# Second row tiles of four experts share one 128-row tile in a sparse attention, mixture-of-experts and feed-forward kernel

## The chip, the cores and the metric

The kernel runs on one core of a Trainium2 chip. The metric is the device time of one execution in microseconds; of several executions the median is given. The engines are named as the profile names them: PE is TensorE, PEld its weight loads, DVE VectorE, ACT ScalarE, POOL GpSimd, SP SyncE; a "q" behind a name is that engine's queue of issues.

## What is computed

```python
attn = attention(q, k, v)            # 4 x 8 heads, 576 positions, 64 wide; half local, half strided
x = attn as [2304, 512]
do = x @ w_skip > 0
e = argmax(x[do] @ w_gate, axis=1)   # 8 experts
gate = softmax(x[do] @ w_gate)[e]
x[do] += gate * (relu(x[do] @ w1[e]) @ w2[e])      # w1: 512 x 1024, w2: 1024 x 512
h = x @ w_in                         # 512 x 2048
out = maximum(0.01 * h, h) @ w_out   # 2048 x 512
```

With the inputs that the reference draws, 1016 of the 2304 rows go to an expert: 113, 110, 157, 141, 148, 152, 107 and 88 for experts 0 to 7.

## The kernel before

There are three stages. In the first, 43 attention units (19 strided, 24 local) go through a pipeline of small steps, one step of the loop for each: scores, exponentials, transposes, products with the values and with the router's weights (`s_scores` to `s_table`). Each row of the result (two halves with their router sums, 530 numbers) goes to DRAM, `x2_d`. From ranks within each expert a table `places` of row numbers is built: 160 places (`CAP`) for each of 8 experts, in two tiles of 128 and 32 (`TS`, `TN`); empty places hold a number out of bounds, and a gather or scatter leaves them out. Idle products (`keep_warm`, on zeros) stand at a few places in PE's order.

In the second stage the experts run one after the other. For each, `gather_rows` fetches the two row tiles by two indirect DMAs on POOL (L636), one expert ahead; `turn_in` (L643) transposes them on PE, four transposes for each tile, and ACT and DVE each copy one half out of PSUM; for eight slices `f` of the hidden width come `first_layer` and, two slices later (`LAG`), `second_layer`, on 160 columns; `copy_out` and `turn_out` (L677) bring the result back, again four transposes for each tile; `expert_out` multiplies it with the gate (`gates`, L619), adds it to the gathered rows and scatters them (L692). Meanwhile DVE, ACT and POOL decode the dense weights, step by step (`decode_tick`). The last expert is joined with the dense layers' start (`last_second` to `last_place`): its rows are put into the first 256 rows' operand by products with a selection matrix, while its scatters and the loads of the next rows (`load_rows`, L611) go on.

In the third stage the dense layers run on tiles of 256 and then 512 rows (`mm1`, `mm2`); a copy and a DMA for each 128 rows bring out the result (L934).

PE's order is the order of the code; on the other engines a scheduler sets it, and `behind_pe` holds an instruction behind another.

Of the kernel before, what the change touches and what calls it, by code (L numbers as in the profile page):

```python
# [36 lines left out]
TS = (slice(0, P), slice(P, CAP))  # L37
TN = tuple(t.stop - t.start for t in TS)
NBLK = -(-(NT - CAP) // CAP)
OC = NBLK * CAP  # L40
# [12 lines left out]
SZ = B * SR - GU * (NSU - 1)  # L53
WARMS = {0: 2, 1: 2, 2: 1}
FC1 = F // P
# [21 lines left out]
WARM_END = 8  # L77
WARM_MID = (4, 1)
VT_LATE = 1
# [20 lines left out]
def tile_sparse_attention_moe_ffn(ctx: ExitStack, tc: tile.TileContext, sb, vs, lb, vl, mk, tris, cst, ranks, wrb, w1, w2, dw, out):  # L100
# [14 lines left out]
    x2_d = dp.tile([NT, XW], F32, name="x2_d")  # L115
    x_parts = dram_disjoint_views(x2_d, 2 * E)

# [88 lines left out]
    acc = const.tile([P, 1, E], BF16, name="acc")  # L206
    idx = const.tile([P, 2, E], U32, name="idx")
    rr_t, m2_t, cm_t = (const.tile([P, NLU], F32, name=n) for n in ("rr_t", "m2_t", "cm_t"))
# [36 lines left out]
    with ExitStack() as actx:  # L245
# [98 lines left out]
        def s_weigh(i):  # L344

            z = st[i]
            nk = z["nk"]
            vw = ps_c.tile([P, 4, P], F32, tag="c", name="vw")[:nk, :2]
            for p in range(2):
                c = (p + (2 if units[i][0] == "s" else 0)) * 2 * NR  # L350
                nc.tensor.matmul(vw[:, p, :NW], z["vt"][:, p, :], wr_sb[:, c:c + NW], start=True, stop=True)  # L351
            ins = nc.scalar.copy(z["v"][:nk, :, D + 1:].rearrange("p (a b) e -> p a b e", a=2),
                                 vw[:, :, :2 * NR].rearrange("p a (b e) -> p a b e", b=2))
            if i < GRP:
                behind_pe(ins, eng=mybir.EngineType.Activation)

# [171 lines left out]
        def s_table(i):  # L528
# [21 lines left out]
            nc.vector.tensor_reduce(places, ix.rearrange("p t a e -> p t e a"), AX.X, ALU.add)  # L550
            nc.vector.tensor_copy(idx, places)

        stages = ((s_scores, 0), (s_load, LL), (s_transpose, 2), (s_weigh, 1),
                  (s_values, 3), (s_join, 3), (s_place, 5), (s_table, 6), (s_logits, 4))
        for step in range(LL, NU + 6):
            for fn, lag in stages:
                if 0 <= step - lag < NU:
                    fn(step - lag)
            keep_warm(WARMS.get(step, 0))
            if step == NU + 2:  # L560
# [55 lines left out]

    gate_of, pairs = {}, {}

    def gates(key, pair):  # L619
        l4 = pair[:, :, :XW].rearrange("p t (h w) -> p t h w", h=2)  # L620
        lg = mp.tile([P, 2, E], F32, tag="glg", name="glg")
        nc.vector.tensor_tensor(lg, l4[:, :, 0, 4 * D:4 * D + E], l4[:, :, 1, 4 * D:4 * D + E], ALU.add)
        nmx = mp.tile([P, 2], F32, tag="gmx", name="gmx")
        nc.vector.tensor_reduce(nmx, lg, AX.X, ALU.max, negate=True)
        nc.vector.tensor_tensor(lg, lg, nmx.unsqueeze(2).to_broadcast([P, 2, E]), ALU.add)
        nc.scalar.activation(lg, lg, AF.Exp)
        es = mp.tile([P, 2], F32, tag="ges", bufs=3, name="ges")
# [3 lines left out]
        gate_of[key] = es  # L631

    def gather_rows(e):
        rows, pairs[e] = row_pair()
        for t, n in enumerate(TN):
            ins = nc.gpsimd.indirect_dma_start(  # L636
                out=rows[t][:n, :XW], out_offset=None, in_=x_parts[2 * e + t][:, :],
                in_offset=bass.IndirectOffsetOnAxis(ap=idx[:n, t, e:e + 1], axis=0),
                bounds_check=NT - 1, oob_is_err=False)
            behind_pe(ins, dep=GDEP)  # L640
        return rows

# [42 lines left out]

    def expert_out(po, rows, toks, gate, e=None):
        for t, n in enumerate(TN):
            ins = nc.vector.scalar_tensor_tensor(x_of(rows[t])[:n], po[t][:n].rearrange("p (h w) -> p h w", h=2),
                                                 gate[:n, t:t + 1], x_of(rows[t])[:n], ALU.mult, ALU.add)
            if e == E - 1:  # L690
                behind_pe(ins)
            nc.gpsimd.indirect_dma_start(  # L692
                out=(x2_d if e is None else x_parts[2 * e + t])[:, :],
                out_offset=bass.IndirectOffsetOnAxis(ap=toks[t], axis=0),
                in_=rows[t][:n, :XW], in_offset=None, bounds_check=NT - 1, oob_is_err=False)
# [11 lines left out]

    def last_turn(po, c2, ot, out):

        (nc.vector.tensor_copy if c2 else nc.scalar.copy)(ot[:, 2 * c2:2 * c2 + 2], po)  # L710
        for t, n in enumerate(TN):
            for c in (2 * c2, 2 * c2 + 1):
                nc.tensor.transpose(out[t][:n, c * P:(c + 1) * P], ot[:, c, TS[t]], ident)

    def last_gate(out, gate, c2, ys):

        cs = slice(c2 * NTT, (c2 + 1) * NTT)
        for t, n in enumerate(TN):
            yh, yl = ys[t]
            nc.scalar.activation(yh[:n, cs], out[t][:n, cs], AF.Identity, scale=gate[:n, t:t + 1])  # L720
            nc.vector.scalar_tensor_tensor(yl[:n, cs], out[t][:n, cs], gate[:n, t:t + 1], yh[:n, cs].bitcast(F32),
                                           ALU.mult, ALU.subtract)

    def last_place(pt, c2, ys, sel, x):

        for c in (2 * c2, 2 * c2 + 1):
            for t, n in enumerate(TN):
                for k, y in enumerate(ys[t]):
                    nc.tensor.matmul(pt[:, c % 2, :], y[:n, c * P:(c + 1) * P], sel[:n, t, :],  # L729
                                     start=False, stop=(t + k == 2 and c % 2 == 1))  # L730
# [20 lines left out]
    LAG = 2  # L751
    rows = {0: gather_rows(0)}
    keep_warm(WARM1)
# [9 lines left out]
    with tc.If(nblk > 0):  # L763
# [24 lines left out]
        with tc.For_i(0, E, 1) as e:  # L788
            with tc.For_i(0, nblk, 1) as k:
# [10 lines left out]
                for f in range(FC1):  # L800
# [4 lines left out]
                    second_layer(gpo, b2, first_layer(b1.rearrange("p (c n) -> p c n", c=KC), gxt), f == FC1 - 1)  # L805
                gates(None, gpair)
                expert_out(turn_out(copy_out(gpo), ps_c, "c"), grows, toks, gate_of.pop(None))

    keep_warm(WARM2)
    xt_of = {0: turn_in(rows[0])}  # L810
    gs, pos, ots = {}, {}, {}
    for j in range(len(seq) + LAG):
        if j < len(seq):
# [9 lines left out]
            if e + 1 < E and f == GF:  # L823
                rows[e + 1] = gather_rows(e + 1)
        for e in list(ots):
            expert_out(turn_out(ots.pop(e), ps_c, "c"), rows.pop(e),
                       [idx[:n, t, e:e + 1] for t, n in enumerate(TN)], gate_of.pop(e), e)
        if LAG <= j < len(seq) + LAG - TAIL:
            e, f = seq[j - LAG]
            second_layer(pos[e], r2s[(j - LAG) // 2][:, f % 2], gs.pop(j - LAG), f == FC1 - 1)  # L830
            if f % 2:
                load_w2((j - LAG) // 2 + 3)
            if f == FC1 - 1:
                ots[e] = copy_out(pos.pop(e))
        if j < len(seq):
            e, f = seq[j]
            if f == 2:
                gates(e, pairs.pop(e))
            if e == E - 1 and f == FC1 - 1:
                sel = mp.tile([P, 2, NTT], F32R, tag="sel", bufs=1, name="sel")  # L840
                for t in range(2):
                    behind_pe(nc.vector.tensor_scalar(sel[:, t, :], rank_sb, places[:, t, E - 1:], None, ALU.is_equal))
            if e + 1 < E and f == 5:
                xt_of[e + 1] = turn_in(rows[e + 1])
    nxt = load_rows(0, dq_last[-1])
    e = E - 1
    po = pos.pop(e)
# [9 lines left out]
    last_second(0, 2)  # L857
    ot = mp.tile([P, KC, CAP], F32, tag="ot", name="ot")
    out_t = [ps_a.tile([P, DM], F32, tag="a", name="pto") for t in TN]
# [3 lines left out]
    last_second(1, 0)  # L863
    last_turn(po[0], 0, ot, out_t)
    last_gate(out_t, gate_of[e], 0, ys)
    pt = turn_next(nxt, 0)
    last_second(1, 2)
    last_place(pt, 0, ys, sel, x0)
    pt = turn_next(nxt, 1)
    last_turn(po[1], 1, ot, out_t)  # L870
    last_gate(out_t, gate_of[e], 1, ys)
    ahead = [open_h(NTT)]
    mm1(ahead[0], 0, x0, (0, 1))
    last_place(pt, 1, ys, sel, x0)
    expert_out(out_t, rows.pop(e), [idx[:n, t, e:e + 1] for t, n in enumerate(TN)], gate_of.pop(e), e)
    ahead.append(open_h(NTT))
# [18 lines left out]
    for j in range(len(fseq) + LAG):  # L895
# [22 lines left out]
        if j >= LAG:  # L918
# [5 lines left out]
            if f == FC2 - 1:  # L924
                po = pos.pop(i)
                for t in ts:
# [9 lines left out]
                    nc.sync.dma_start(out[a:a + P, :], y)  # L936
        if j < len(fseq):
# [145 lines left out]
```

## Time and profile before

| | us |
|---|---|
| median of 3 runs | 695.44 |
| the runs | 693.45, 695.44, 696.0 |
| the profiled execution | 693.17 |
| its span, first to last instruction | 691.1 |
| PE busy | 684.9 |
| attention, until about | 117 |
| experts, about | 123 to 272 |
| dense layers, from about | 288 |

Busy time is read against the stage it lies in: an engine that is half busy over the span can be full in one stage. A transpose or product has a record with its whole latency, so the distance from one group's start to the next says what a group costs; the chain of waits gives these distances. An idle stretch is told with the event that ended it.

### The profile page before, as it was taken

The page shows a single profiled execution, that of the slowest core. Times are in us where ns is not written, and L with a number is a line of the kernel's source. Part 1 is how long each engine was busy: PE and PEld are TensorE (multiplying, and loading weights), DVE is VectorE, ACT ScalarE, POOL GpSimd, SP SyncE. Part 2 cuts the span into 40 slices and gives each one's busy share as a digit, 9 for nine tenths or more (in the row PEclk, how much of TensorE's full clock was granted, in tenths as well). Part 3 has the DMA queues.
Part 4 walks back from the last instruction along what each step waited for, and adds up shares of the span by engine and source line. Part 5 has one row for each costly group of instructions (what it writes and reads, how often), then busy time and mean ns, then how long its engine had stood idle before and what let it go on. Part 6 is the DMA issues. An engine that isn't in the chain of part 4 may idle for free.

```text
span 691.1 us, 11591 instructions
## 1 busy us (share of the span) xinstructions
PE 684.9 (99%) x4336; PEld 596.5 (86%) x4336; DVE 334.4 (48%) x971; ACT 259.9 (38%) x685; POOL 115.3 (17%) x170
## 2 busy tenths in 40 slices
PE   9999999999999999999999999999999999999997
PEld 6999986899999999888888888888888888888886
DVE  4788886244445553589988322223222232222221
ACT  5677763223323333355545223223232222232222
POOL 1333323133333332123332000000000000000000
PEclk9999999999999999999999999999999999999999
DMA  8978772688898887253332021000110000010001
GB/s 324 357 252 277 243 291 59 204 285 296 298 308 292 299 292 264 75 194 115 107 96 57 0 94 62 0 1 1 31 38 24 1 1 0 1 61 1 1 0 61
DMA packets 36558, 92.71 MB, mean 134 GB/s; under 512 B 6016, under 2 KB 8160, under 8 KB 36496
## 3 DMA queue, kind: packets, MB, share of 16 engines
q1 hardware_dynamic: 31568, 82.79, 35.6%
q0 software_dynamic: 4640, 8.99, 4.0%
q8 instruction: 35, 0.57, 0.3%
q14 instruction: 27, 0.22, 0.1%
q10 hardware_dynamic: 288, 0.13, 0.1%
HBM read 80.69 MB, written 12.32 MB: 135 GB/s over the span
## 4 chain that ended last, share of the span: by engine, by line
PE 97%; DVE 1%; issue 1%; DMA 0%; ACT 0%; POOL 0%; POOLq 0%; DVEq 0%; ACTq 0%
PE ph L743 28%; PE pf L749 28%; PE ph L656 10%; PE po L669 9%; PE o L384 5%; PE pt L362 3%; PE vw L351 3%; PE sc L334 3%; PE sc L331 2%; PE ptx L596 1%; PE pto L682 1%; PE ptx L648 1%; PE pw L219 1%; PE po L853 1%; PE pts L729 0%
## 5 line engine op out<-in xcount | busy, mean ns | idle before, releaser
L749 PE MATMUL pf<-wouth,gp 128*128 128x512 f32 x576 | 190.5, 390 | 0.0
L910 DVE TENSOR_TENSOR tg<-tg,ph 128x512 f32<-128x512 f32 (+1 forms) x80 | 50.7, 633 | 171.6 <-ACT tg L909 171.5
L749 PEld LDWEIGHTS pf<-wouth,gp 128*128 128x128 f32 x576 | 108.2, 188 | 22.2 <-DVE gp L916 0.2
L743 PE MATMUL ph<-th,winh 128*128 128x512 f32 (+1 forms) x320 | 119.4, 373 | 0.0
L743 PE MATMUL ph<-tl,winh 128*128 128x512 f32 (+1 forms) x320 | 118.1, 369 | 0.1
L743 PE MATMUL ph<-th,winl 128*128 128x512 f32 (+1 forms) x320 | 118.0, 369 | 0.0
L749 PE MATMUL pf<-woutl,gp 128*128 128x512 f32 x288 | 112.3, 390 | 0.0
L909 ACT ACTIVATE tg<-ph 128x512 f32<-128x512 f32 (+1 forms) x80 | 44.2, 553 | 178.2 <-PE ph L743 178.1
L656 PE MATMUL ph<-xt,r 128*128 128x160 f32 x512 | 80.6, 301 | 0.4 <-ACT xt L650 0.3
L669 PE MATMUL po<-g,r 128*128 128x160 f32 x480 | 75.0, 299 | 0.0
L656 PEld LDWEIGHTS ph<-xt,r 128*128 128x128 f32 x512 | 72.7, 190 | 1.5 <-ACT xt L650 0.7
L916 DVE TENSOR_TENSOR gp<-tg,gp 128x512 fp32r<-128x512 f32 (+1 forms) x80 | 51.0, 638 | 42.7 <-ACT gp L915 42.6
L743 PEld LDWEIGHTS ph<-th,winh 128*128 128x128 f32 x320 | 60.3, 188 | 10.7 <-DVE tl L598 0.4
L743 PEld LDWEIGHTS ph<-tl,winh 128*128 128x128 f32 x320 | 60.3, 189 | 10.4 <-DVE tl L734 0.3
L743 PEld LDWEIGHTS ph<-th,winl 128*128 128x128 f32 x320 | 60.3, 188 | 10.1
L669 PEld LDWEIGHTS po<-g,r 128*128 128x128 f32 x480 | 68.3, 190 | 0.1
L915 ACT CAST gp<-tg 128x512 fp32r<-128x512 f32 (+1 forms) x80 | 46.1, 578 | 50.7 <-DVE tg L910 50.3
L749 PEld LDWEIGHTS pf<-woutl,gp 128*128 128x128 f32 x288 | 54.1, 188 | 10.7
L340 ACT ACTIVATE p_t<-sc,mx 96x128 f32<-96x128 f32 (+2 forms) x172 | 48.3, 361 | 10.9 <-DVE mx L337 8.2
L658 ACT ACTIVATE g<-ph 128x160 f32<-128x160 f32 x64 | 19.2, 301 | 60.1 <-PE ph L656 60.1
L384 PE MATMUL o<-vt,pts 128*96 128x104 f32 (+4 forms) x344 | 39.6, 258 | 0.1
L151 ACT ACTIVATE w<-raw 128x256 f32<-128x256 f32 x64 | 27.8, 434 | 29.6 <-POOL woutl L169 18.9
(130 smaller groups left out, 774.9 us busy)
## 6 DMA issues: line engine op xcount, KB each, us to landing
r<-in_w SPq DMA_DIRECT2D x64, 512.0 KB, 4.7
raw<-in_dw SPq DMA_DIRECT2D x64, 256.0 KB, 4.1
gt<-in_lb SPq DMA_DIRECT2D x12, 704.0 KB, 6.3
gt<-in_sb SPq DMA_DIRECT2D x7, 756.0 KB, 6.6
row<-x_d SPq DMA_DIRECT2D x9, 530.0 KB, 4.5
out<-ys SPq DMA_DIRECT2D x18, 256.0 KB, 2.1
vt<-in_vl SPq DMA_DIRECT2D x12, 296.0 KB, 6.3
vt<-in_vs SPq DMA_DIRECT2D x9, 296.0 KB, 5.7
```

The source lines that it names most:

```text
L151: behind_pe(nc.scalar.activation(wf, raw[:, :, 1].bitcast(F32), AF.Abs))
L334: nc.tensor.matmul(sc[:, a, p], z["q"][r, p], z["k"][r, p], start=False, stop=p == 1)
L340: nc.scalar.activation(p_t[:nq, h, :nk], sc[:, h % 2, h // 2], AF.Exp, bias=mx[:, h % 2, h // 2:h // 2 + 1], scale=scale)
L384: nc.tensor.matmul(o[:nq, h, :w], z["pts"][:nk, h, :nq], z["v"].rearrange("p a b -> p (a b)")[:nk, h * VP:h * VP + w], start=True, stop=True)
L656: nc.tensor.matmul(ph, w[:, c, :], xt[:, c, :], start=c == 0, stop=c == KC - 1)
L669: nc.tensor.matmul(po[c // 2][:, c % 2], w[:, c * P:(c + 1) * P], g, start=False, stop=end and c % 2 == 1)
L743: nc.tensor.matmul(ph, dense_w[k, f][:, c, :], v[:, c % 2], start=c + i == 0, stop=c == KC - 1 and i == 2)
L749: nc.tensor.matmul(po[t], a[:, s], x, start=(first and i == 0), stop=(last and i == 2))
L909: nc.scalar.mul(t1, ph, 0.01)
L910: ins = nc.vector.tensor_tensor(g, t1, ph, ALU.max)
L915: nc.scalar.copy(gh, g)
L916: nc.vector.tensor_tensor(gl, g, gh.bitcast(F32), ALU.subtract)
```

## The change

The second tiles of four experts become one tile of 128 rows, each expert with 32 of them (`EG`, `NG`, `SEC`): `gidx` holds its row numbers, made by four small products from `places` and a cast. The first expert of a group gathers it, transposes it and keeps the transposed rows (`xg`); each expert's operand gets a slice of 32 columns by a copy. Behind the second layer, the last 32 columns go into `otg`, which is transposed back, multiplied with its gates and scattered behind the group's last expert. Fixed places (`SLOTS`, `GSLOTS`) hold the rows. Of the idle products those of steps 1 and 2 (`WARMS`) and one ahead of the last table products (`WARM_MID`) go, one is added ahead of the small products; those of step 0 use another pool. The copy of the router's products (`s_weigh`) isn't held behind ACT's last instruction any more. The gates are held behind PE. The last copy of the kernel is made in two halves, on DVE and ACT, each with its own DMA.

```diff
+EG = 4
+NG = E // EG
+SEC = CAP - P
+SLOTS = (0, 2, 3, 4, 0, 2, 3, 4)
+GSLOTS = (1, 5)
...
-WARMS = {0: 2, 1: 2, 2: 1}
+WARMS = {0: 2}
...
-WARM_MID = (4, 1)
+WARM_MID = (4, 0)
...
-            if i < GRP:
-                behind_pe(ins, eng=mybir.EngineType.Activation)
...
-            nc.vector.tensor_copy(idx, places)
+            nc.vector.tensor_copy(idx, places[:, 0])
+            keep_warm(1, ps_s, "s")
+            gi = ps_b.tile([P, NG], F32, tag="b", name="gi")
+            for k in range(EG):
+                nc.tensor.matmul(gi[k * SEC:(k + 1) * SEC], ident[:SEC, :SEC],
+                                 places[:SEC, 1].rearrange("p (g k) -> p k g", k=EG)[:, k], start=True, stop=True)
+            nc.vector.tensor_copy(gidx, gi)
+            nc.scalar.copy(gplaces, gi)
...
+    def gather_rows(e):
+        gather(slot(SLOTS[e]), idx[:, e:e + 1], e)
+        g = e // EG
+        if e % EG == 0:
+            gather(slot(GSLOTS[g]), gidx[:, g:g + 1], E + g)
+
+    def turn(rows):
+        pt = ps_c.tile([P, KC, P], F32, tag="c", name="ptx")
+        for c in range(KC):
+            nc.tensor.transpose(pt[:, c], rows[:, x_cols(c)], ident)
+        return pt
...
+    def turn_rows(e):
+        xt = mp.tile([P, KC, CAP], F32, tag="xt", name="xt")
+        pt = turn(slot(SLOTS[e]))
+        g, k = divmod(e, EG)
+        if k == 0:
+            pg = turn(slot(GSLOTS[g]))
+            nc.vector.tensor_copy(xt[:, :, P:], pg[:, :, :SEC])
+        nc.scalar.copy(xt[:, :2, :P], pt[:, :2])
+        nc.vector.tensor_copy(xt[:, 2:, :P], pt[:, 2:])
+        if k == 0:
+            xgs[g] = mp.tile([P, KC, P], F32, tag="xg", name="xg")
+            nc.vector.tensor_copy(xgs[g][:, :, SEC:], pg[:, :, SEC:])
+        else:
+            nc.vector.tensor_copy(xt[:, :, P:], xgs[g][:, :, k * SEC:(k + 1) * SEC])
+        return xt
...
+    def put_out(e, c2, po, ot):
+        g, k = divmod(e, EG)
+        if k == 0 and c2 == 0:
+            otgs[g] = mp.tile([P, KC, P], F32, tag="otg", bufs=1, name="otg")
+        a, b = (nc.scalar.copy, nc.vector.tensor_copy)[::-1 if c2 else 1]
+        cs = slice(2 * c2, 2 * c2 + 2)
+        a(ot[:, cs], po[:, :, :P])
+        b(otgs[g][:, cs, k * SEC:(k + 1) * SEC], po[:, :, P:])
...
+        while done:
+            e, ot = done.pop(0)
+            rows_out(turn_back(ot), slot(SLOTS[e]), idx[:, e:e + 1], e, e)
+            g, k = divmod(e, EG)
+            if k == EG - 1:
+                rows_out(turn_back(otgs.pop(g)), slot(GSLOTS[g]), gidx[:, g:g + 1], E + g, E + g)
...
-                    nc.scalar.copy(y, po[t])
+                    if end and t == ts[-1]:
+                        cs = slice(0, NTT), slice(NTT, DM)
+                        nc.vector.tensor_copy(y[:, cs[0]], po[t][:, cs[0]])
+                        nc.sync.dma_start(out[a:a + P, cs[0]], y[:, cs[0]])
+                        nc.scalar.copy(y[:, cs[1]], po[t][:, cs[1]])
+                        nc.scalar.dma_start(out[a:a + P, cs[1]], y[:, cs[1]])
```

The order of PE where expert 0's result is turned back, between products of expert 1 (`ph` is the first layer, `po` the second, `pto` the transposes; an `r_` is a weight tile), before:

```order
L656 MATMUL ph<-xt,r_2928 128x160 x4
L682 MATMUL pto<-ident,ot 128x128 x4
L682 MATMUL pto<-ident,ot 32x128 x4
L669 MATMUL po_2964<-g,r_2913 128x160 x2
L669 MATMUL po_2965<-g,r_2913 128x160 x2
```

and with the change:

```order
L724 MATMUL ph<-xt,r_2928 128x160 x4
L699 MATMUL pto<-ident,ot 128x128 x4
L737 MATMUL po_2964<-g,r_2917 128x160 x2
L737 MATMUL po_2965<-g,r_2917 128x160 x2
L724 MATMUL ph<-xt,r_2928 128x160 x4
```

Four of the eight transposes are gone; where expert 3 is turned back, four of `otg` stand in their place. The transposes in (`ptx`) lose their four of 32 rows in the same way.

The order of PE at the end of attention, where the last table products (`ix`) are closed and idle products (`pw`) follow, with the change (before, the rows of `gi` and one pair of `pw` aren't there):

```order
L551 MATMUL ix<-oa,rm 32x16
L554 LDWEIGHTS zero
L554 MATMUL ix<-zero 128x32
L226 LDWEIGHTS zero
L226 MATMUL pw<-zero 128x512
L560 MATMUL gi<-places,ident 32x2 x4
L226 LDWEIGHTS zero
```

The four products of `gi` stand ahead of the twelve idle products that cover the gathers, and wait for `places`.

The order of DVE around the transposes into expert 1 (`w` are decoding steps), before:

```order
L162 SCALAR_TENSOR_TENSOR w<-raw,w 128x256
L650 COPY xt<-ptx 128x320
L156 TENSOR_SCALAR w<-w 128x256
L160 TENSOR_SCALAR w<-w 128x256
L161 SCALAR_TENSOR_TENSOR w<-raw,w 128x256
L162 SCALAR_TENSOR_TENSOR w<-raw,w 128x256
```

and with the change:

```order
L161 TENSOR_SCALAR w<-w 128x256
L677 COPY xt<-ptx 128x2x128
L165 TENSOR_SCALAR w<-w 128x256
L166 SCALAR_TENSOR_TENSOR w<-raw,w 128x256
L167 SCALAR_TENSOR_TENSOR w<-raw,w 128x256
L682 COPY xt<-xg 128x4x32
```

The operand's copy is smaller and stands behind one decoding step more; the slice of the group's rows comes four steps behind that.

## Rows read from the trace of the kernel before

**Rows 1.** The page: busy time with share and instructions; granted clock by slice.

```profile
PE 684.9 (99%) x4336; PEld 596.5 (86%) x4336; DVE 334.4 (48%) x971; ACT 259.9 (38%) x685; POOL 115.3 (17%) x170
...
PEclk9999999999999999999999999999999999999999
```

**Rows 2.** Stage table: stretch, length, busy time per engine, granted clock, DMA share, GB/s.

```profile
123.00:272.00 149.00, 148.64 (x1109) 145.52 (x1108) 73.65 (x199) 45.91 (x144) 47.98 (x56) 1.00 0.84 285
```

**Rows 3.** Chain of work, 136 to 157 us: start, length, engine, line.

```profile
136.56 1.28 PE ph L656 x8
...
146.81 0.87 PE pto L682 x8
147.68 1.09 PE po L669 x8
...
155.29 0.80 PE ptx L648 x8
156.09 1.01 PE ph L656 x6
```

**Rows 4.** Waits of PE's weight loads, 117 to 272 us: in total, times, longest.

```profile
PEld ptx L648 <- issue: 1.3, 8, 0.2
```

**Rows 5.** Opening: timeline of weight loads and one DMA issue, then that issue's landing.

```profile
7.77 0.13 PEld L331 LDWEIGHTS <-mk_sb 64*126 64x126 bf16 x2 [0.42 <-DVE mx L337]
...
9.50 0.12 PEld L219 LDWEIGHTS <-zero 128*128 128x128 bf16 x1
10.08 0.13 PEld L331 LDWEIGHTS <-mk_sb 64*126 64x126 bf16 x2 [0.46 <-issue]
...
12.63 0.13 PEld L331 LDWEIGHTS <-mk_sb 64*126 64x126 bf16 x2
...
5.48 0.36 SPq L292 DMA_DIRECT2D gt<-in_sb  x1
...
gt<-in_sb SPq DMA_DIRECT2D x1, 756.0 KB, 6.6
```

**Rows 6.** Chain of work, its first piece.

```profile
1.00 3.17 PE pw L219 x7
```

**Rows 7.** Turn to the experts: timeline of POOL and PEld, then both gathers' landings.

```profile
118.68 1.13 POOL L636 DMA_INDIRECT row<-x_d,idx  x1 [2.24 <-issue]
120.12 0.94 POOL L636 DMA_INDIRECT row<-x_d,idx  x1 [0.31 <-issue]
...
124.34 0.57 PEld L656 LDWEIGHTS ph<-xt,r 128*128 128x128 f32 x4 [0.68 <-ACT xt L650]
125.16 0.98 PEld L656 LDWEIGHTS ph<-xt,r 128*128 128x128 f32 x7 [0.26 <-DVE xt L650]
...
row<-x_d,idx POOLq DMA_INDIRECT x1, 3.8
...
row<-x_d,idx POOLq DMA_INDIRECT x1, 2.8
```

**Rows 8.** Into the dense layers: timeline; landings of two scatters, one row load.

```profile
287.16 0.88 POOL L692 DMA_INDIRECT x_d<-row,idx  x1 [0.30 <-DVE tl L734]
...
289.14 1.43 SPq L611 DMA_DIRECT2D row<-x_d  x3
...
294.56 1.02 PEld L596 LDWEIGHTS ptx<-ident,row 128*128 128x128 f32 x8
...
x_d<-row,idx POOLq DMA_INDIRECT x1, 2.7
...
x_d<-row,idx POOLq DMA_INDIRECT x1, 1.9
...
row<-x_d SPq DMA_DIRECT2D x1, 530.0 KB, 4.8
```

**Rows 9.** The end: timeline of ACT; and the group of ACT's 256-column copies.

```profile
687.47 0.58 ACT L934 COPY ys<-pf 128x512 f32<-128x512 f32 x1 [0.72 <-PE pf L749]
...
L733 ACT CAST th<-pts 128x256 fp32r<-128x256 f32 x2 | 0.7, 372 | 2.4 <-PE pts L729 1.9 <-DVE tl L734 0.5
```

More of the change, by code (lines that the diff above doesn't have):

```diff
@@ L558, in tile_sparse_attention_moe_ffn @@
                     fn(step - lag)
-            keep_warm(WARMS.get(step, 0))
+            keep_warm(WARMS.get(step, 0), ps_b, "b")
             if step == NU + 2:
@@ L630, in gates @@
         nc.vector.reciprocal(es, es)
-        gate_of[key] = es
-    def gather_rows(e):
[L634 to L641, printed above, removed]
+        gate_of.update((k, es[:, t:t + 1]) for t, k in enumerate(keys))
@@ new lines, in slot, with gather @@
+    def slot(i):
+        return row_pairs[i // 2][:, i % 2]
+    def gather(r, tok, part):
+        ins = nc.gpsimd.indirect_dma_start(
+            out=r[:, :XW], out_offset=None, in_=x_parts[part][:, :],
+            in_offset=bass.IndirectOffsetOnAxis(ap=tok, axis=0), bounds_check=NT - 1, oob_is_err=False)
+        behind_pe(ins, dep=GDEP)
+    def gather_rows(e):
+        gather(slot(SLOTS[e]), idx[:, e:e + 1], e)
+        g = e // EG
+        if e % EG == 0:
+            gather(slot(GSLOTS[g]), gidx[:, g:g + 1], E + g)
@@ new lines, in tile_sparse_attention_moe_ffn, with turn_back @@
+    otgs = {}
+    def put_out(e, c2, po, ot):
[6 more added lines that the diff above has]
+        b(otgs[g][:, cs, k * SEC:(k + 1) * SEC], po[:, :, P:])
+    def turn_back(ot):
+        p = ps_c.tile([P, DM], F32, tag="c", name="pto")
+        for c in range(KC):
+            nc.tensor.transpose(p[:, c * P:(c + 1) * P], ot[:, c], ident)
+        return p
@@ L643, in turn_in, with rows_out @@
+    def rows_out(p, r, tok, key, part, last=False):
+        ins = nc.vector.scalar_tensor_tensor(x_of(r), p.rearrange("p (h w) -> p h w", h=2), gate_of.pop(key),
+                                             x_of(r), ALU.mult, ALU.add)
+        if last:
+            behind_pe(ins)
+        nc.gpsimd.indirect_dma_start(
+            out=x_parts[part][:, :], out_offset=bass.IndirectOffsetOnAxis(ap=tok, axis=0),
+            in_=r[:, :XW], in_offset=None, bounds_check=NT - 1, oob_is_err=False)
     def turn_in(rows):
@@ L684, in turn_out, with expert_out @@
         return po
-    def expert_out(po, rows, toks, gate, e=None):
+    def expert_out(po, rows, toks, gate):
         for t, n in enumerate(TN):
[L688 to L691, printed above, removed]
+            nc.vector.scalar_tensor_tensor(x_of(rows[t])[:n], po[t][:n].rearrange("p (h w) -> p h w", h=2),
+                                           gate[t][:n], x_of(rows[t])[:n], ALU.mult, ALU.add)
             nc.gpsimd.indirect_dma_start(
-                out=(x2_d if e is None else x_parts[2 * e + t])[:, :],
-                out_offset=bass.IndirectOffsetOnAxis(ap=toks[t], axis=0),
+                out=x2_d[:, :], out_offset=bass.IndirectOffsetOnAxis(ap=toks[t], axis=0),
                 in_=rows[t][:n, :XW], in_offset=None, bounds_check=NT - 1, oob_is_err=False)
@@ L751, in tile_sparse_attention_moe_ffn @@
     LAG = 2
-    rows = {0: gather_rows(0)}
+    gather_rows(0)
     keep_warm(WARM1)
@@ L833, in tile_sparse_attention_moe_ffn @@
             if f == FC1 - 1:
-                ots[e] = copy_out(pos.pop(e))
+                ot = mp.tile([P, KC, P], F32, tag="ot", name="ot")
+                for c2, p in enumerate(pos.pop(e)):
+                    put_out(e, c2, p, ot)
+                done.append((e, ot))
         if j < len(seq):
@@ L837, in tile_sparse_attention_moe_ffn @@
             if f == 2:
-                gates(e, pairs.pop(e))
+                if e == 0:
+                    gates((0, E), row_pairs[0])
+                else:
+                    gates((e,), slot(SLOTS[e]).unsqueeze(1))
+            if f == 3 and e and e % EG == 0:
+                gates((E + e // EG,), slot(GSLOTS[e // EG]).unsqueeze(1))
             if e == E - 1 and f == FC1 - 1:
                 sel = mp.tile([P, 2, NTT], F32R, tag="sel", bufs=1, name="sel")
-                for t in range(2):
-                    behind_pe(nc.vector.tensor_scalar(sel[:, t, :], rank_sb, places[:, t, E - 1:], None, ALU.is_equal))
+                for t, at in enumerate((places[:, 0, E - 1:], gplaces[:, NG - 1:])):
+                    behind_pe(nc.vector.tensor_scalar(sel[:, t, :], rank_sb, at, None, ALU.is_equal))
             if e + 1 < E and f == 5:
-                xt_of[e + 1] = turn_in(rows[e + 1])
+                xt_of[e + 1] = turn_rows(e + 1)
     nxt = load_rows(0, dq_last[-1])
+    gate = gate_of[E - 1], gate_of[E + NG - 1]
     e = E - 1
@@ L863, in tile_sparse_attention_moe_ffn @@
     last_second(1, 0)
-    last_turn(po[0], 0, ot, out_t)
-    last_gate(out_t, gate_of[e], 0, ys)
+    last_turn(po[0], 0, ots, out_t)
+    last_gate(out_t, gate, 0, ys)
     pt = turn_next(nxt, 0)
@@ L874, in tile_sparse_attention_moe_ffn @@
     last_place(pt, 1, ys, sel, x0)
-    expert_out(out_t, rows.pop(e), [idx[:n, t, e:e + 1] for t, n in enumerate(TN)], gate_of.pop(e), e)
+    rows_out(out_t[0], slot(SLOTS[e]), idx[:, e:e + 1], e, e, last=True)
+    rows_out(out_t[1], slot(GSLOTS[NG - 1]), gidx[:, NG - 1:], E + NG - 1, E + NG - 1, last=True)
     ahead.append(open_h(NTT))
```

71 lines of the change are left out of this document (36 added, 35 removed).

## The prediction

> **What bounds the kernel now.** I read the page first. TensorE (PE) is busy for 99% of the span, and the granted clock is in its top tenth in all 40 slices [rows 1]. The chain of waits that ended last runs through PE's instructions, one behind the other, as its piece in [rows 3] shows. So time is lost or won where PE works, and only there; the other engines count where PE waits for them. Next the stage table: while the experts run (123 to 272 us) PE is busy for 148.64 of 149 us, VectorE (DVE) for 73.65, ScalarE (ACT) for 45.91, and the DMA engines for 0.84 of theirs at 285 GB/s [rows 2]. The reader should see that PE is full, DVE and ACT are about half idle or more, and the DMA engines are the only other resource that is near its end. Then the chain inside one expert: from one expert's first product after its transposes (136.56) to the next one's (156.09) it takes 19.53 us, without a gap [rows 3].
>
> **The change part by part.** The experts get 113, 110, 157, 141, 148, 152, 107 and 88 rows, so the second row tiles hold 0, 0, 29, 13 and 20, 24, 0, 0: a group tile carries 42 rows, then 44.
>
> *Transposes back.* Eight take 0.87 us, for both tiles, so four take 0.435 [rows 3]. Experts 0, 1, 2, 4, 5 and 6 now turn back one tile; 3 and 7 still two. Saved: 6 x 0.435 = 2.61 us.
>
> *Transposes in.* Eight take 0.80 us, and the eight products behind them 1.28 us until the next group starts (136.56 to 137.84), where a group of eight otherwise takes 1.09 (147.68): 0.99 in all [rows 3]. The extra 0.19 I lay to the 32-row tile: the weight loads of these transposes wait eight times for "issue", 1.3 us together, which is once for each expert, where the operand changes from 128 rows to 32 [rows 4]. With four 128-row transposes left (0.435) an expert saves 0.555; six of them (1, 2, 3, 5, 6, 7) save 3.33. Expert 4 has eight of 128 rows: 0.99 - 0.87 = 0.12. If the 0.19 stays, it is 6 x 0.365 - 0.07 = 2.12 instead of 3.45.
>
> So the experts' stage gives 6.06 us (at least 4.73). What is added there is covered: the group copies, an extra copy on each engine for every expert, lie on DVE and ACT, and the 32-row multiply-add on DVE goes. The transposed rows are wanted only after the layers 6 and 7, 4 x 1.09 us later; without that cover each late microsecond would cost PE one. POOL loses one gather and one scatter for six of eight experts.
>
> *Opening.* Three idle products go. Those of step 1 cost nothing, since PE waits for the scores' buffer anyway. That of step 2 stands between 9.50 and 10.08, with its load of 0.12 and 0.46 us of "issue" behind it: 0.58 [rows 5]. But the scores of unit 4 start at 12.63, and their operands, issued at 5.48, land 6.6 us later, at 12.08 [rows 5]: 0.55 us is the most. I take 0.45, as the semaphore needs some of it; the lower end is 0.
>
> *The turn to the experts.* One idle product ahead of the last table products goes; a 512-column product took 3.17 / 7 = 0.45 us at the start, at the 1.2 GHz level [rows 6], so 0.2 at 2.4 GHz, and the gathers go out 0.2 earlier. Added are one idle product and four small products that build the group's indices (on PE, then a cast on DVE); POOL is busy with the first gather until 119.81 and issues the second at 120.12, so this wait is covered. The first gather carries 113 rows and lands 3.8 us after its start; the second carried no row and landed after 2.8 [rows 7]. Now it carries 42: 2.8 + 42/113 = 3.2 us, so 123.1 with the 0.2. Then four transposes (0.435), their own length (0.2) and a small DVE copy (0.3, estimates): the first layer starts at about 124.1. Before, it started at 124.34, waited for DVE's half of the copy until 125.16 and finished 0.54 later, at 125.70 [rows 7]; the gate's work stood ahead of that copy and now stands behind it. New end: 124.1 + 1.09 = 125.2, a gain of 0.5. Bounds: 3.8 us for the gather gives -0.1, 2.8 us gives 0.7 (PE's own idle products then set the start).
>
> The Trainium skill ("DMA: Bandwidth & Descriptors", Anatomy of one DMA) prices a GpSimd transfer at 2.0 us and its bytes at 436 GB/s; 42 rows of 2,120 bytes would be 0.2 us in place of my 0.4, and with the same for the scatter below the time would come out at 688.1.
>
> *Into the dense layers.* The last scatter moved no row: issued at 287.16, it landed 1.9 us later, and the row loads go out at once behind it, at 289.14. The second of them, just after 289.6, takes 4.8 us, so 294.45; PE loads its first transpose at 294.56 [rows 8]. The slack is 0.1. Now the scatter carries 44 rows; one of 88 rows took 2.7 us: 1.9 + 0.8 x 44/88 = 2.3, and PE stalls for 0.3. Bounds: 0 and 0.7.
>
> *The end.* The last copy takes 0.58 us on ACT; 256 columns take 0.37 [rows 9]. Halves on two engines and two queues: 0.2 earlier (0 to 0.4).
>
> Sum: -6.06 - 0.45 - 0.5 - 0.2 + 0.3 = -6.9 us (-3.9 to -7.7). The profiled execution took 693.17 us (span 691.1, 2.1 around it), 2.3 below the median of the runs shown. From it the sum gives 686.3; from the median of 695.44, 688.5. I forecast the median: **688.5 us**.
>
> **The rivals.** *The clock falls in the opening.* Fewer idle products leave PE idle for over half a microsecond near 7 us, just when it has become fast. For it speaks that the first seven products run at 0.45 us [rows 6]; against it that PE is full from then on and no slice shows a lower clock [rows 1]. If the low level came back for as long as these seven took (3.2 us), half of that, 1.6 us, would be lost: 690.1, still faster. The Trainium skill ("TensorE: Matmul & The Clock Gate", Part 1) says that the clock is halved after idleness and restored by sustained work, which speaks for keeping such products; no run here shows it as yet.
>
> *The DMA engines become the experts' bound.* They are at 0.84 [rows 2]; weights for an expert must come in 18.5 us and not 19.5, so 0.89. If 285 GB/s were all that this mix of transfers gives, the 6.06 would be kept back by waits for weights, and only the -0.85 of the other terms is left: 694.6, no change. Against it: no weight load is named by any PE wait.
>
> *The change does less than it says:* the saved transposes come back as waits for the copies of group rows, in part, and 2 to 3.4 us remain: 692 to 693.4, no change to measure.
>
> *Slower: the slice copy holds up each expert.* DVE's copy of a slice into the next expert's operand stands in its queue behind decoding steps, which wait for ACT and for their loads. From 4.6 us behind the transposes (4 x 1.09 and the two zero products) each microsecond is PE's. For a loss over 3.5 us seven experts would have to stall for 1.5 us each, so the copy would have to come 6.1 us late: 699. Against it: DVE is idle for half of the stage [rows 2].
>
> **How the numbers follow.** About 0.5% (3.5 us) can be told from no change here. My forecast has 0.80, the clock 0.05, the DMA bound 0.06, the weak form 0.06, the slice copy 0.03. Faster: 0.80 + 0.05 = 0.85; same: 0.12; slower: 0.03. The range goes from 693.17 - 7.7 = 685.5 to 695.44 - 3.9 = 691.5; it holds the first two cases, and leaves out about 0.15.
>
> **What would show it.** Right: the chain from expert to expert at 18.5 us where no group is turned, the group of eight products behind the transposes at 1.09; the first layer done near 125 us; unit 4's scores near 12.2 us; a PE wait of about 0.3 us ahead of the transposes near the start of the dense layers; PE's idle products short by three. Wrong: weight loads for the experts waiting on a DMA (the second rival), weight loads of the first layer waiting for a copy on DVE (the fourth), idle products at double length after 7 us (the first), or the transposes' saving coming out at 4.7 because the 0.19 is not the 32-row tile's.

## The result and the profile after

The changed kernel takes **687.85 us** (median of 6, 687.62 to 688.41) where the kernel before, in the same group of runs, takes 694.57 (median of 6, 692.76 to 696.0): a ratio of 0.9913, 95% interval 0.99 to 0.9927. In a second group it was 688.05 to 693.50, 0.9923 (0.991 to 0.9936). So 5.5 to 6.7 us are gained; 6.9 were forecast. The time itself came out 0.65 us below the forecast 688.5 because the kernel before was 0.9 faster here than the 695.44 that the forecast started from; the gain is 0.2 to 1.5 us smaller than forecast. The profiled execution took 688.41 us with a span of 686.64, 4.43 less than the 691.07 before; it is the slowest of its six, so the sums below are made span against span.

The page of the profile, busy time and granted clock (to compare with [rows 1]); then the stage table of the experts (stretch, length, busy time of PE, PEld, DVE, ACT and POOL, clock, DMA share, GB/s; to compare with [rows 2]):

```profile
PE 678.5 (99%) x4293; PEld 592.4 (86%) x4293; DVE 333.4 (49%) x991; ACT 261.6 (38%) x695; POOL 105.4 (15%) x158
...
PEclk9999999999999999999999999999999999999999
...
123.00:268.00 145.00, 144.50 (x1075) 143.13 (x1073) 70.58 (x216) 47.27 (x152) 38.34 (x45) 1.00 0.86 294
```

PE is still full, and the DMA engines deliver 294 GB/s where they delivered 285: they were not the bound. The chain inside an expert, where no group tile is turned (to compare with [rows 3]):

```profile
136.86 0.44 PE ptx L664 x4
137.30 1.09 PE ph L724 x8
...
147.36 0.44 PE pto L699 x4
147.79 1.09 PE po L737 x8
...
155.40 0.44 PE ptx L664 x4
155.84 1.09 PE ph L724 x8
```

155.84 - 137.30 = 18.54 us, where 18.5 was forecast and 19.53 was before; four transposes for eight in both places, and the group behind the transposes takes 1.09, no longer 1.28.

Waits of PE's weight loads over the span, the ones that are new or belong to a term:

```profile
PEld ptx L608 <- DMA row<-x_d: 1.1, 1, 1.1
...
PEld ph L724 <- ACT xt L676: 0.8, 1, 0.8
...
PEld sc L341 <- DMA gt<-in_sb: 0.7, 1, 0.7
...
PEld gi L560 <- DVE places L555: 0.4, 1, 0.4
```

No weight load of the experts is in that view behind the first group (`ph L724` is the one at the turn). What is in it stands in the opening, at the end of attention (`gi`), at the turn to the experts, and at the second dense tile's rows.

Cut at six events on PE (start of the last table product; the first first-layer group; the last products of expert 7, L853/L928; the first product of the dense second layer; the first 512-column product; the last product), the two spans compare so:

| stretch | before | after | difference | forecast |
|---|---|---|---|---|
| to the last table product (opening, one idle product) | 117.19 | 116.84 | -0.35 | -0.65 |
| from there to the first group (turn) | 7.15 | 8.92 | +1.77 | -0.3 |
| to the last products of expert 7 | 150.16 | 143.76 | -6.40 | -6.06 |
| expert 7's turn, gate and placing | 16.04 | 14.94 | -1.10 | none |
| into the dense layers | 8.73 | 9.79 | +1.06 | +0.3 |
| dense layers | 387.78 | 387.98 | +0.20 | none |
| last product to the end | 4.02 | 4.41 | +0.39 | -0.2 |
| span | 691.07 | 686.64 | -4.43 | -6.9 |

(The +0.20 of the dense layers lies within the spread of the grouped kernels, 387.68 to 388.45. Before, the first group had a hole of 0.27 in it, from its missing half [rows 7]; it counts to the turn: there +1.50, and -6.13 for the experts.) The one stretch of which the prediction says nothing is expert 7's placing. PE's timeline there, first of the kernel before, then of the change (start, busy, line, product, rows by columns):

```profile
280.28 0.39 PE L729 MATMUL pts<-sel,yh 128*128 128x256 f32 x1
280.51 0.28 PE L729 MATMUL pts<-sel,yl 128*128 128x256 f32 x1
280.71 0.38 PE L729 MATMUL pts<-sel,yh 32*128 32x256 f32 x1
280.94 0.27 PE L729 MATMUL pts<-sel,yl 32*128 32x256 f32 x1
...
282.00 0.39 PE L700 MATMUL pts<-zero 128*128 128x512 bf16 x1
```

```profile
275.30 0.39 PE L792 MATMUL pts<-sel,yh 128*128 128x256 f32 x1
275.53 0.28 PE L792 MATMUL pts<-sel,yl 128*128 128x256 f32 x1
275.64 0.28 PE L792 MATMUL pts<-sel,yh 128*128 128x256 f32 x1
275.76 0.28 PE L792 MATMUL pts<-sel,yl 128*128 128x256 f32 x1
...
276.36 0.39 PE L765 MATMUL pts<-zero 128*128 128x512 bf16 x1
```

The same eight products take 1.72 us with operands of 128 and 32 rows in turn, and 1.06 with 128 throughout. With one height they follow each other at 0.11 to 0.12 us behind the first; where pairs of 128 and 32 rows alternate, every step takes 0.20 to 0.23 us, those inside a pair too.

### The profile page after: what moved, and what is told of

It is laid out like the page before. It is cut to its first block, busy times and chain, and to the rows that moved or that the text cites. A ratio compares the mean times of both kernels' runs of the same rounds, so it can differ in the third digit from the quotient of the medians.

```text
span 686.6 us, 11504 instructions
## 1 busy us (share of the span) xinstructions
PE 678.5 (99%) x4293; PEld 592.4 (86%) x4293; DVE 333.4 (49%) x991; ACT 261.6 (38%) x695; POOL 105.4 (15%) x158
## 4 chain that ended last, share of the span: by engine, by line
PE 77%; DMA 3%; issue 2%; DVE 0%; POOL 0%; ACT 0%; SPq 0%; POOLq 0%
PE pf L812 28%; PE ph L806 28%; PE ph L724 9%; PE po L737 9%; DMA row<-x_d 1%; PE ptx L608 1%; DMA x_d<-row,idx 1%; PE ptx L664 1%; PE pto L699 1%; DMA x_d<-row,gidx 0%; PE po L732 0%; PE pw L226 0%; POOL x_d L707 0%; DVE row L703 0%; SPq L623 0%
## 5 line engine op out<-in xcount | busy, mean ns | idle before, releaser
L724 PE MATMUL ph<-xt,r 128*128 128x160 f32 x512 | 79.6, 299 | 0.5 <-DVE xt L675 0.5
L724 PEld LDWEIGHTS ph<-xt,r 128*128 128x128 f32 x512 | 72.7, 190 | 1.1 <-ACT xt L676 0.8
L174 POOL TENSOR_TENSOR winl<-w,winh 128x256 fp32r<-128x256 f32 x32 | 25.2, 788 | 91.6 <-ACT winh L173 91.5
```

The source lines that it names most:

```text
L174: nc.gpsimd.tensor_tensor(lo, wf, hi.bitcast(F32), ALU.subtract)
L724: nc.tensor.matmul(ph, w[:, c, :], xt[:, c, :], start=c == 0, stop=c == KC - 1)
```

## The experiments

Three groups, each with the kernel before on the same chip (693.37, 693.50 and 693.17 us, medians of 11, 17 and 11). The change itself was run again in the second.

> The change itself again, so that the other kernels of this group have it beside them on the same chip. Theory (what two executions of the same edits differ by is the opening's loads and the clock at the turn, under 1 us together): 0.9915 of the kernel before, as in its first comparison (0.9913), and the granted clock from 117 to 123 us either 1.00 or near 0.72. Rival (the first comparison's 6.7 us held an accident of the kernel before, whose profiled execution was only 4.8 us slower): 0.993 to 0.994.

688.05 us, 0.9923: between the two; its interval (0.991 to 0.9936) holds the theory's 0.9915 and a part of the rival's range, so neither is ruled out. The granted clock from 117 to 123 us was 0.72 again.

**The grouping alone.** Opening, idle products and last copy as before:

```diff
-WARMS = {0: 2}
+WARMS = {0: 2, 1: 2, 2: 1}
...
-WARM_MID = (4, 0)
+WARM_MID = (4, 1)
```
and `nc.scalar.copy(y, po[t])` with one store for the last copy; the pool of step 0's idle products and the order of the router's copy are put back too.

> The grouping alone: opening, idle products and last copy as before. Theory: the grouping is all of the gain. From one profiled pair: experts -6.1 (from the first layer's first group to the last products), the last expert's placing products -1.1 (no 32-row operand among them), turn to the experts +0.6 (the group's gather lands near 123.7 us, no low clock), stall on the row loads of the second dense tile +1.1. Sum -5.5, so 694.6 - 5.5 = 689.1 us, 1.3 above the change. Rival: the other edits are worth nothing together (opening -0.1, removed product +0.9 or nothing, halves +0.3), and this kernel stands within 0.4 us of the change, 687.5 to 688.3, or below it.

688.45 us (688.18 to 688.52), 0.9928 (0.9915 to 0.9941): 4.9 us gained. The change didn't run in this group; its medians elsewhere are 687.85 and 688.05, and the intervals overlap. 688.45 lies between the theory's 689.1 and the rival's 688.3, and the times decide for neither. The stretches of its span from the last table product on are 8.93, 143.76, 14.96 and 10.17, the change's but for the entry into the dense layers. So the grouping carries the gain, and the other edits together are worth little: by the traces below the opening gives about 0.6 us, and the halved last copy takes 0.4 back.

**The idle product back.** The stage table ahead of it, 117 to 123 us, shows a clock of 0.72 for the change, and 1.00 for the kernel before:

```profile
117.00:123.00 6.00, 5.64 (x26) 2.09 (x25) 0.52 (x3) 0.16 (x1) 2.17 (x2) 0.72 0.25 66
```

```diff
-WARM_MID = (4, 0)
+WARM_MID = (4, 1)
```

> The change with its one idle product ahead of the last table products put back. Theory (the clock fell at the turn because that product is gone): granted clock 1.00 from 117 to 123 us instead of 0.72, the twelve idle products behind the table at about 0.22 us each instead of 0.43, the transposes of the first gathered rows start near 122.7 instead of 123.7, the first layer's first group ends near 126.0 instead of 126.85; time 687.0 us (0.9 below the change). Rival (the group's gather, which lands at 123.5, sets the end of the turn at either clock, and the product only shifts it): the clock comes back, but the group ends at 126.9 or later and the time is 687.9 to 688.1. Second rival (the clock does not depend on that product): still 0.7 to 0.8 of full clock there, 688.0.

688.48 us (0.994, 0.9919 to 0.9961), and the same low clock: the twelve idle products take 4.45 us, at the level of 1.2 GHz for most of that time (2.75 us in the kernel before, at 2.4).

```profile
117.00:123.00 6.00, 5.70 (x19) 2.08 (x18) 0.15 (x1) 0.16 (x1) 2.17 (x2) 0.72 0.25 66
...
116.85 4.45 PE L226 MATMUL pw<-zero 128*128 128x512 bf16 x12
```

The theory falls: that product alone does not hold the clock. The fall does not belong to the change alone either: the kernel before with full-height transposes (below) shows 0.77 in the same stretch. In all profiled executions with a fall at the turn the mean clock of the span is 0.998 or lower, in those without one 0.999 or 1.000; it is 0.998 or lower in 12 of 39 executions of the kernel before, in 9 of the change's 11, and in 4 of 6 here. Why the grouping makes it likelier was not settled; the weight loads' wait of 0.36 us for `places` and the four small products (eight in the trace) ahead of the idle ones are new there, but the full-height kernel fell without them.

**The last copy whole.** The edit is the last part of the first experiment's.

> The change with its last copy whole on ScalarE and one store, as before. Theory (in the change ScalarE's half stands behind VectorE's half: 683.11 after 682.65 + 0.42, so the halves follow one another): the copy ends 1.00 us after the last product's start instead of 1.25, the store of twice the bytes lands 0.3 later after its issue; from last product's start to the span's end 4.05 us as in the kernel before instead of 4.37; time 687.5 us (0.3 below the change). Rival (the prediction's term, halves save 0.2): 688.0 us.

687.13 us (686.54 to 688.52), 0.9914 (0.9901 to 0.9927); from the last product to the end 4.02 us, in the grouping alone 4.01, where the change has 4.41. The theory holds by the trace; by the times alone it would not be told from the change. It is the fastest kernel of this study, but its interval overlaps the change's. This execution also kept the full clock at the turn, and so shows what else sets it. Its chain of work there (start, length, what):

```profile
119.15 4.38 DMA row<-x_d,gidx
...
123.67 0.64 PE ptx L664 x4
...
124.33 0.30 DVE xt L675
...
124.77 3.50 PE ph L724 x24
```

At the full clock the turn takes 8.54 us (8.37 in the run with the old opening), against 8.92 at the low one: the low clock costs 0.4 to 0.55 us. At the full clock PE awaits the group's gather. In the change's own profile, at the low one, it does not: that gather went out at 119.76 and landed 3.7 us later, at 123.46, while PE was still at its idle products. The chain there:

```profile
122.23 1.89 PE pw L226 x8
124.11 0.45 PE ptx L664 x4
...
124.59 0.38 ACT xt L676
...
124.99 0.07 DVE xt L677
...
125.34 0.29 DVE xt L675
...
125.76 1.32 PE ph L724 x8
```

So the idle products that cover the gathers end too late there, and behind the transposes three copies follow one another: ScalarE's half, VectorE's half (`L677`, 0.42 us), then the group's slice (`L675`). The gather sets the turn at the full clock, the idle products and these copies at the low one.

**The opening as before.** `WARMS`, the pool of step 0's idle products and the order of the router's copy are put back, and nothing else.

> The change with the opening's three idle products and the order of ScalarE's copy put back. Theory (unit 4's scores wait for a load whose landing does not move): scores of unit 2 start at about 10.1 instead of 9.2, those of unit 4 at 12.6 instead of 12.53, and the last table product is 0.1 to 0.15 us later; time 688.0 us. Rival (the prediction's term): 0.45 later, 688.3 us.

688.74 us, 0.9939 (0.9926 to 0.9952); unit 4's scores at 13.13, the last table product at 117.46. The theory, taken from one pair, falls. Over all profiled executions the last table product starts at 117.19, 117.18 and 116.70 (mean 117.0) where the old opening and the product stand, and at 115.98 to 116.99 (nine, mean 116.4) with the change's: 0.6 us, near the prediction's 0.65. The opening carries it: with the product alone put back the start is at 116.21, no later than the nine.

**The halves in two tiles.**

```diff
+y2 = rw.tile([P, 2, NW2], F32R, tag="r1", bufs=3, name="y2")[:, 0, :NTT].bitcast(F32)
+nc.scalar.copy(y[:, cs[0]], po[t][:, cs[0]])
+nc.vector.tensor_copy(y2, po[t][:, cs[1]])
...
```

The two engines change places, and the stores follow.

> The change with the two halves of its last copy in different tiles. Theory (ScalarE's half waits for VectorE's because both write one tile): the halves run beside each other, both are done 0.85 us after the last product's start instead of 1.25, and from that start to the span's end it takes 3.9 us instead of 4.37 (the kernel before: 4.05): 0.45 us below the change. Rival (the halves wait for one another because both read the same buffer of the product): they still follow one another, and the end stays at 4.3 to 4.4 us.

The timeline of the change's last copies, and of this kernel's:

```profile
682.23 0.39 PE L812 MATMUL pf<-wouth,gp 128*128 128x512 f32 x1
682.65 0.42 DVE L1013 COPY ys<-pf 128x256 f32<-128x256 f32 x1 [5.40 <-PE pf L812]
...
683.11 0.37 ACT L1015 COPY ys<-pf 128x256 f32<-128x256 f32 x1 [1.18 <-DVE ys L1013]
```

```profile
682.50 0.37 ACT L1014 COPY ys<-pf 128x256 f32<-128x256 f32 x1 [0.72 <-PE pf L812]
...
682.90 0.42 DVE L1015 COPY y<-pf 128x256 f32<-128x256 f32 x1 [5.81 <-ACT ys L1014]
```

688.38 us (0.9931, 0.9918 to 0.9944), end 4.38: the second half waits for the first also where they write different tiles. The rival holds: what they have in common is the product's buffer, which both read. The transposes into an expert show the same thing the other way round. The kernel before has two buffers for them, and its two copies run beside each other though they write one tile; the change has one buffer, and they follow each other (first before, then the change):

```profile
156.00 0.42 ACT L650 COPY xt<-ptx 128x320 f32<-128x320 f32 x1 [1.46 <-PE ptx L648]
156.13 0.49 DVE L650 COPY xt<-ptx 128x320 f32<-128x320 f32 x1 [1.95 <-PE ptx L648]
```

```profile
155.88 0.37 ACT L676 COPY xt<-ptx 128x256 f32<-128x256 f32 x1 [1.22 <-PE ptx L664]
...
156.28 0.42 DVE L677 COPY xt<-ptx 128x256 f32<-128x256 f32 x1 [2.62 <-ACT xt L676]
```

The Trainium skill ("PSUM — Partial Sum Buffer", PSUM bank collisions raise a hardware error) says that two engines must not read one bank's same 32 partitions at once, and that the compiler therefore puts a dependency between them; both orders in these traces agree with that. A split by partitions, which that section would allow, was not run.

**One group more of lead for the second dense tile.**

```diff
-LEAD = 4
+LEAD = 5
```

> The change with the second dense tile's rows wanted one group of hidden columns later (lead of 5 for 4). Theory (TensorE stalls because the scatter of 128 rows lands about 1 us later than the one of 32 and the row loads go out behind it): the wait on the row load at the transposes, 1.06 us in the change, is gone, nothing else on TensorE changes: 0.8 to 1.1 us below the change. Rival (what is late is the decoding of the dense weights or another operand, and the stall only moves): a wait of about the same size at other products of the dense layers, and the time of the change within 0.3 us.

688.10 us (687.0 to 692.79), 0.9934 (0.9912 to 0.9957). Its waits of weight loads, from the last expert on, begin so:

```profile
PEld ptx L608 <- DVE tl L610: 0.8, 2, 0.6
PEld ph L806 <- DVE tl L610: 0.6, 1, 0.6
```

The wait on the row load is gone, so the first part of the theory holds; in its place come 0.8 us in which the transposes wait for VectorE to free their buffer. From the first product of the dense second layer to the last product it takes 397.24 us, where the change has 397.77 and 398.20: 0.5 to 1.0 less by the trace, nothing that the times show.

**The kernel before with full-height transposes.**

```diff
-nc.tensor.transpose(pts[c // 2][:, c % 2, TS[t]], rows[t][:n, x_cols(c)], ident[:n, :n])
+nc.tensor.transpose(pts[c // 2][:, c % 2, t * P:(t + 1) * P], rows[t][:, x_cols(c)], ident)
```

> The kernel before, with the second tile's transposes in taken over all 128 partitions of its buffer instead of 32 (the further columns that come out are not used). This tells what a change of operand height costs by itself. Theory (each change between 128 and 32 rows costs TensorE 0.19 us): the eight transposes take 0.87 us instead of 0.80, the eight products behind them 1.09 instead of 1.28, the expert's period 19.4 instead of 19.53; over eight experts 1.0 us below the kernel before. Rival (the 0.19 us is the wait of the new expert's first products for something else, a copy or a buffer): 1.28 stays, the transposes cost 0.07 more each time, 0.5 us above the kernel before.

692.71 us (11 runs), 0.9988 (0.9979 to 0.9997), with the chain as the theory has it:

```profile
135.54 0.87 PE ptx L648 x8
136.42 1.09 PE ph L656 x8
...
154.95 0.87 PE ptx L648 x8
155.83 1.09 PE ph L656 x8
```

19.41 us for an expert: four transposes have four times the rows, and the expert is still 0.12 us shorter. So the change of height costs, and not a wait for a copy or a buffer. The placing of expert 7 keeps its 32-row operands in this kernel, and its 16.04 us.

**The first two groups split**, 128 columns ahead of the group tile's transposes, 32 behind:

```diff
+for f in range(2):
...
+    for c in range(KC):
+        nc.tensor.matmul(ph[:, :P], r1s[0][:, f, c], xt[:, c, :P], start=c == 0, stop=c == KC - 1)
...
 pg = turn(slot(GSLOTS[g]))
```

Expert 0's own rows then come by one copy on ScalarE, not by two halves.

> The change, with the first two first-layer groups of expert 0 made in two parts: 128 columns as soon as that expert's own rows are turned, and the 32 columns from the group tile behind the group's transposes. Theory (the landing of the group's gather sets the end of the turn, and TensorE has 1.3 to 2 us to spare ahead of it): the eight products of 128 columns lie in the time in which TensorE waited; behind the group's transposes there are eight products of 32 columns, about 0.85 us, in place of 2.18: the stretch from the last table product to the last products of the experts, 152.3 us at the full clock in the change with a whole last copy and 152.7 at the low one, becomes 151.0 to 151.6, and the time 1.0 us less than the change's. Rival (the transposes and copies of expert 0's own rows set the end, not the landing): no gain, since the first parts start as late as the groups did and the weights are loaded twice: 0.3 to 0.8 us above the change.

690.21 us, 0.9949 (0.9932 to 0.9967): about 2 us slower than the change, beyond the rival too. From the last table product to the last products of expert 7 it takes 154.66 us where the change takes 152.68, both at the low clock; at the full clock it is 153.21 (the last run of the combined ones) for 152.30 (whole copy), so the split costs 0.9 us there too. The chain:

```profile
124.82 2.05 PE ph L678 x16
126.87 0.45 PE ptx L664 x4
...
127.69 3.14 PE ph L738 x24
```

Two groups of 128 columns take 2.05 us; then two of 32 columns and one of 160 take 3.14, so a 32-column group costs 1.0, as much as one of 128. I had priced it at 0.42. The Trainium skill ("TensorE: Matmul & The Clock Gate", Back-to-back issue gap) has the spacing of products set by the weight load as well as by the columns; the rows agree. PE stands in order, and the group's transposes queued behind these 2 us.

**Combined:** split, whole copy, and the lead of 5 or 4.

> The change with the split first groups, the last copy whole and the lead of 5. Theory (the three losses of the change are at three different places and add up): 1.0 from the turn, 0.35 from the end, 0.5 from the entry into the dense layers: 1.8 us below the change, a ratio to the kernel before of 0.9895. Rival (the place of one is taken by a wait for another): under 1 us below the change, 0.991.

> The same without the lead of 5. Theory: 1.35 us below the change, with the wait of 1.0 to 1.1 us on the second dense tile's row load still there; 0.9902 of the kernel before. Rival (the lead of 5 is worth nothing, as its own comparison, 688.10 against 688.05, has it): as fast as the kernel with the lead of 5, within 0.2 us.

688.82 us, 0.993 (0.991 to 0.995), and 689.52, 0.9944 (0.9926 to 0.9963): neither beats the change, since the split takes more than the other two bring.

**Group tiles without rows.** `gidx` is `gi` plus 8192.

> The change with all 128 indices of the group tiles out of range, so that their gathers and scatters move no row: it leaves out the second tiles' rows. Theory of the prediction (landing grows with the rows that are moved): the group's first gather lands 2.8 us after its start, as the empty one of 32 indices did, instead of 3.4 to 4.4, and the last scatter after 1.9 instead of 2.9; the stall at the second dense tile is 0.1 us or none. Rival (it grows with the number of indices, whether a row is moved or not): 3.4 to 4.4 and 2.7 to 2.9 stay, and so does the stall of about 1 us.

Landing of its group gather, and its last scatter in the chain:

```profile
row<-x_d,gidx POOLq DMA_INDIRECT x1, 3.6
...
282.66 2.87 DMA x_d<-row,gidx
```

The time, 690.16 us in one execution, says little: its clock at the turn was the lowest of all (0.50 from 117 to 123 us). The rival holds by the landings, and the wait on the row load stays too (1.9 us there). A gather of 128 indices lands after 3.6 us with no row, after 3.4 to 4.4 with 42 in the other executions; the last scatter after 2.87 with none, 2.7 to 2.9 with 44. The empty ones of 32 indices took 2.8 and 1.9 [rows 7, 8]. So the number of indices counts at these two places, and not the rows. The other traffic counts too: while an expert's weights come in, empty gathers of 32 indices in the kernel before took 4.2 to 4.7 us.

## Why the prediction was right, and where not

*Transposes back and in:* right in mechanism and size. 6.06 was forecast, 6.13 measured; every kernel with the grouping and undivided first groups has 143.76 us for the experts' stretch. The operand-height penalty, on which 1.3 us of it hung, is shown by itself (the full-height transposes).

*Missed:* the same penalty in expert 7's placing products, worth 1.1 us. The prediction saw the 32-row operand at the transposes and did not look for it elsewhere. That this gain met the unforeseen losses is luck.

*Opening and removed product:* 0.6 us of 0.65, but all of it in the opening, which was to give 0.45; no run shows the product's 0.2. Unit 4's scores were forecast near 12.2: those on the mask start at 11.73, but those that need the load at 12.53, behind a wait for it. The profiled pair alone showed half of the 0.6; one pair is too little where loads of 6 to 7 us land at other times in each execution.

*Turn:* wrong in sign. "2.8 + 42/113 = 3.2 us" failed: landing goes with indices, not with rows, and 3.4 to 4.4 was measured; without any row it is 3.6. Behind the landing, transposes, copy and handovers take 1.24 us (123.53, where the gather lands, to 124.77 in the whole copy's chain) where I had 1.0. That makes a loss of 1.0 to 1.1 us at the full clock, outside the bound of 0.1 (which took 3.8 us for the gather). At the low clock the loss is 1.5, and there the step that failed is another: the idle products, which the prediction let set the start only at a gather of 2.8 us, end behind the landing, and the copies follow one another in place of the one of 0.3.

*Into the dense layers:* the wait was forecast, its size was off: "1.9 + 0.8 x 44/88 = 2.3" measured 2.85, and the stall 1.06 in place of 0.3, above the bound of 0.7 (1.0 to 2.0 in the other executions with this lead). The scatter, the row loads behind it and PE's loads for the transposes:

```profile
281.51 2.85 DMA x_d<-row,gidx
...
284.51 1.49 SPq L623 DMA_DIRECT2D row<-x_d  x3
...
288.61 0.24 PEld L608 LDWEIGHTS ptx<-ident,row 128*128 128x128 f32 x2 [0.17 <-issue]
289.92 0.64 PEld L608 LDWEIGHTS ptx<-ident,row 128*128 128x128 f32 x6 [1.06 <-DMA row<-x_d]
```

The longer scatter is the smaller part. Counted from the start of expert 7's last products (274.50 before, 269.52 now), the scatter is issued 0.67 us earlier and the row loads go out 0.35 later (14.99 for 14.64). PE comes to the first of these transposes 1.0 us earlier (19.09 for 20.06), because the placing is shorter. So most of the stall is the placing's gain taken back, at a load that does not come sooner.

*End:* wrong in sign. "Halves on two engines" do not run beside each other; the last copy ends 1.25 us after the last product's start in place of 1.00, and the end comes 3.16 us behind it in place of 3.02.

*The rivals:* no wait for weights and no wait for the slice copy appeared. The clock did not fall in the opening (1.00 from 4 to 8 us), but at the turn, where no case had it. The Trainium skill ("TensorE: Matmul & The Clock Gate", Part 1) says that the clock is halved after idleness, which spoke for keeping idle products. No run here shows idleness as the cause: in the change's profile the clock fell while PE's longest idle stretch from 100 us on was 0.25 us, and putting the product back did not prevent it.

So the total came out right with the main term. In the profiled pair it is 4.4 of 6.9: the turn is 1.8 us worse than forecast, the entry 0.8, the end 0.6, the opening 0.3 and the dense layers 0.2, and 1.1 of unforeseen gain stands against that. The medians give 5.5 to 6.7, as the change's profiled execution is its slowest and that of the kernel before was faster than its median.

## What to carry to other kernels

Tiles of a few rows cost TensorE twice, in fixed cost per product and at each change of operand height: put the small remainders of several units into one tile of full height, and look for every place where the short operand is read. An indirect transfer is to be priced by its indices and by the traffic beside it, not by the rows that it moves. Work saved ahead of a load's landing comes back as a wait if the load does not go out sooner. Halving a copy between two engines gains nothing while both read the same buffer of a product.

## What was not expected of the hardware

- Products of 256 columns follow each other at 0.12 us with one operand height, at 0.20 to 0.23 where pairs of 128 and 32 rows alternate; a first-layer group behind 32-row transposes takes 0.19 us more.
- A first-layer group of 32 columns takes 1.0 us, one of 128 columns 1.0, one of 160 columns 1.09.
- An indirect transfer of 128 indices without a valid row lands in 3.6 us (gather) and 2.87 us (scatter), as one with rows does; the empty ones of 32 indices took 2.8 and 1.9 at the same places.
- Two copies out of one product's buffer by VectorE and ScalarE followed each other (0.42 and 0.37 us) in both orders; out of two buffers into one tile they ran beside each other, 0.13 us apart.
- The granted clock at one place of one and the same program differed between executions: the mean over the span was 0.998 or lower in 12 of 39 of the kernel before.
